# A gated long convolution and token MLP on one core: the k·v branch ahead of the filter, separate shuffle places, and a new fixed order

## The chip, the core and the metric

The kernel runs on one core of a Trainium2 chip. The core has a matrix engine (TensorE, PE), three engines for elementwise work (VectorE or DVE, ScalarE or ACT, GpSimd or POOL) and a sync engine (SP) that here only issues DMAs. The engines share an on-chip memory (SBUF, here one tensor named `arena`) and take matmul results from PSUM (`ps`, eight banks). Every engine runs its own list of instructions in a fixed order; semaphores hold an instruction until what it needs is done. The metric is device time in microseconds.

## The reference

The input x = A_q is 2048 tokens by 448 channels in bf16. Two blocks follow one another, each with a residual connection.

```python
# block A, on q = layernorm(x)
k_shift = sum over t in 0..3 of shift(k, t) * shift_k[:, t]     # causal, 4 taps, per channel
kv = k_shift * v
y  = irfft(rfft(kv, 4096) * rfft(ssm_k, 4096))[:2048]           # causal convolution of length 2048, per channel
h  = x + q * (y + kv * ssm_D)
# block B, over the tokens
u  = gelu(einsum("bsd,sf->bdf", layernorm(layernorm(h)), w1) + b1)   # f = 1792
out = h + transpose(einsum("bdf,fs->bds", u, w2) + b2)
```

## The kernel before

**The long convolution** is a Fourier transform of 4096 points (odd frequencies) written as matmuls. Tokens lie as 128 partitions by 16 rows. Both `kv` (the "u" branch) and the filter `ssm_k` (the "k" branch) go through the same steps:

1. *Stage 1* (`emit_stage1`, matmuls L1049): 16 steps per branch, each eight 32-row matmuls with a table `E` into two PSUM banks, then one eviction of 128 x 896 elements by ACT or DVE (L1059; L1057 for the first k group, which also adds `ssm_D`). The eviction writes a staging place (`GR_`). Four steps fill one place.
2. *Shuffle*: after every second step three DMAs (L1065; two issued by POOL, one by SP) carry the staged data to other partitions, into `TK` for k or `TU` for u.
3. *Stage 2* (`emit_stage2`, matmuls L1084) with the table `FW`; evictions L728, L729, L731, L732 write `TK` or `TU` in place.

Then `emit_products_i1` forms four products per frequency on DVE (L1150) and the first inverse stage on PE (L1167), evicted again by L728 and L731. DMAs L1190 shuffle the result into `TZ`. `emit_i2` (L1289, L1297) ends the inverse transform, gates with the normalised q, adds up statistics and writes the normalised rows `Q`. The MLP follows: L1422 is the first matmul for 7 of 14 column blocks, L1432 for the other 7 (ACT applies gelu, L1412), L1444 the second matmul, row by row, with L1447 on DVE and output DMAs L1452 to L1458.

**What feeds the two branches.** The k branch needs the filter's four channel chunks (load L877 into `KN`) transposed by PE (L1028) and evicted into `KT`. The u branch needs all of k (L888), transposed (L956) and evicted into `KX`; a short convolution on PE (L982) with a table `DG`, which DVE makes (L941) from the shift weights (loads L880 and L883, cast on POOL L934); and v (L891), which DVE multiplies in (L997). The table `E` is made on DVE (L827 product, L831 add, L834 mask) and ACT (sine, L837), in two halves of eight rows. The q path loads X (L905), takes statistics on DVE (L1226, L1228) and the reciprocal root on POOL (L1234, L1237).

**Places.** Four staging places form a ring, `gring`; the eight groups of the two branches take them as they come free. Two of them lie where X goes later and two where the product buffers (`MR`) go. X is loaded after all shuffles of u. The filter, `KN`, lies in the place of `TU`.

**What sets the order.** The program is planned when it is built. Every helper records its operations with a list of what they read and write. Each step, such as "stage 1 of u, step 5", takes a rank from the table `WHEN`. A list scheduler with an estimated duration for each operation then walks through time: whenever an engine is free it takes, among the operations that are ready, the one with the smallest rank. `WHERE` says for an eviction whether ACT (a), DVE (d) or either (f) may do it. The result is one fixed order per engine, and the waits are put in from the recorded reads and writes. A DMA is an operation of the queue that issues it, so an issue that waits holds what stands behind it.

Of the kernel before, what the change touches and what calls it, by code (L numbers as in the profile page):

```python
# [7 lines left out]
ALU = mybir.AluOpType  # L8
# [4 lines left out]
    "dummy": (54,),  # L13
    "tables": (137, 107, 179, 164, 70, 80, 73, 176,),
    "loads": (106, 111, 114, 115, 217, 195, 86, 237, 90, 235, 158, 197, 227, 143, 150,),
    "kv": (219, 110, 132, 216, 134, 214, 55, 208, 233, 84, 103, 104, 75, 127, 138, 154, 196,),
    "kT": (60, 57, 218, 64, 231, 198, 146, 78,),
    "k1": (109, 112, 145, 186, 105, 136, 139, 157, 61, 89, 100, 135, 92, 207, 161, 159,),
    "k2": (85, 88, 67, 87, 129, 141, 98, 155, 206, 203, 173, 175, 102, 113, 185, 247,),
    "u1": (68, 81, 99, 116, 131, 147, 144, 169, 172, 174, 210, 229, 65, 97, 140, 223,),  # L20
    "xload": (287, 46, 43, 49,),
    "bias": (193, 277,),
    "q": (213, 278, 298, 222, 309, 50, 94, 204, 279,),
    "u2": (72, 83, 209, 220, 156, 192, 82, 63, 96, 151, 149, 133, 53, 56, 291, 221,),
    "ew": (244,),
    "i1": (272, 29, 45, 194, 122, 263, 123, 91, 128, 273, 148, 265, 71, 74, 38, 189, 126,),
    "ct0": (188, 288,),
    "ct": (225, 3, 302,),
    "xn": (5, 17, 93, 39, 125, 261,),
    "w1a": (205, 303, 163, 286,),  # L30
    "warm": (41, 2,),
    "i2": (304, 9, 299, 58, 124, 22, 66, 234, 79, 305, 1, 160, 108, 23, 13, 310, 21, 42, 162, 6, 202, 10, 120, 18,
        69, 295, 19, 184, 27, 20, 142, 101, 306, 292, 34, 32, 255, 11, 165, 51, 289, 153, 224, 200, 301, 52, 187,
        177, 238, 199, 269, 280, 300, 226, 259, 118, 180, 31, 7, 170, 215, 117, 166, 167, 276, 181, 232, 307, 33,
        296, 4, 76, 77, 14, 182, 283, 168, 30, 293, 95, 47, 152, 12, 183, 270, 28, 37, 16, 40, 171, 36, 308, 44, 239,
        130, 15, 62, 119, 212, 228, 274, 24, 258, 25, 59, 35,),
    "w1b": (211,),
    "w2": (249,),
    "mlp": (190, 240, 8, 178, 297, 26, 48, 201, 290, 230, 121, 0, 241, 243, 275, 242, 260, 294, 418, 419, 420, 421,
        422, 423, 424, 425, 426, 427, 428, 429, 430, 431, 432, 433, 434, 435, 436, 437, 438, 439,),  # L40
}
WHERE = {
    "kv": "ddaadfdd",
    "kT": "ddfdfddd",
    "k1": "faffaffadfaa",
    "k2": "addfffdaffdafffd",
    "u1": "fafdffafafddfffa",
    "bias": "f",
    "u2": "aadafafafaaaffaf",
    "i1": "aaaaffafaaafaffa",  # L50
    "ct0": "d",
    "ct": "fda",
    "xn": "ffff",
    "i2": "afffaaffddfd",
# [89 lines left out]
class _Sched:  # L144
# [161 lines left out]
    def schedule(self):  # L306
# [70 lines left out]
        while done < n:  # L377
            progressed = False
            for e in ENGS:
                if free_at[e] <= t + 1e-9 and ready[e]:  # L380
# [34 lines left out]
                    if o.is_dma:  # L415
                        d0 = free_at[e] + (1200.0 if o.rate != 425.0 else 2000.0)
                        s = max(d0, fab)
                        fab = s + o.nbytes / o.rate
                        fin = max(fab, s + o.nbytes / (o.keng * 27.2))
                        fin += 600.0  # L420
                    else:
                        fin = free_at[e] + self.lat[e]
# [150 lines left out]
def _build(nc, A_q, A_k, A_v, A_shift_k, A_ssm_k, A_ssm_D, B_w1, B_b1, B_w2, B_b2, out):  # L573
# [36 lines left out]
    o_KN = o_TU  # L610
# [17 lines left out]
    with ctx:  # L628
# [53 lines left out]
        o_GR = (o_WR, o_WR + 8 * DB, o_X, o_X + 8 * DB)  # L682

        def GR_(s):
            return view(o_GR[s], [R // 4, 2, D])
# [13 lines left out]
        gring = _Pool(4)  # L699
# [9 lines left out]
        def Pbf(b, i, dt_=bf16):  # L709
            return PS[:, b.slots[i], :].bitcast(dt_)  # L710
# [26 lines left out]
        def emit_tables():  # L737
# [85 lines left out]
            for h in range(2):  # L823
                sch.t0 = T_TH if h else -40.0
                o_ph = (o_pi, o_TK)[h]
                ph = view(o_ph, [2, 8, 128], i32)
                op("dve", lambda e, W, h=h, ph=ph: e.tensor_tensor(  # L827
                    out=ph[:, 1], in0=frow.unsqueeze(1).broadcast_to([128, 8, 128]),
                    in1=srow[:, 8 * h:8 * h + 8].unsqueeze(2).broadcast_to([128, 8, 128]), op=ALU.mult),
                   r=[(o_fr, 512), (o_s, 64)], w=[(o_ph + 4096, 4096)], n=HALF, kind="1x")  # L830
                op("dve", lambda e, W, ph=ph: e.tensor_scalar(  # L831
                    out=ph[:, 0], in0=ph[:, 1], scalar1=2048, scalar2=None, op0=ALU.add),
                   r=[(o_ph + 4096, 4096)], w=[(o_ph, 4096)], n=HALF)
                op("dve", lambda e, W, ph=ph: e.tensor_scalar(  # L834
                    out=ph, in0=ph, scalar1=8191, scalar2=None, op0=ALU.bitwise_and),
                   r=[(o_ph, 8192)], w=[(o_ph, 8192)], n=2 * HALF)
                op("act", lambda e, W, h=h, ph=ph: e.activation(  # L837
                    out=E[:, 16 * h:16 * h + 16, :].rearrange("p a (b c f) -> p a b c f", b=4, c=2).rearrange("p a b c f -> p (a b) c f"),
                    in_=ph.rearrange("p c r (g f) -> p c (r g) f", f=16).rearrange("p c g f -> p g c f"),
                    func=ACT.Sin, bias=bias[:, 0:1], scale=-SC),  # L840
                   r=[(o_ph, 8192), (o_b, 4)], w=[(o_E + 4096 * h, 4096)], n=2 * HALF)
# [31 lines left out]
        def emit_loads():  # L873
            Dq = "sp"
            for i, c in enumerate((0, 1, 2, 3)):
                sch.t0 = -20.0 + i
                op(Dq, lambda e, W, c=c: e.dma_start(KN[0:CW[c], c, :], A_ssm_k[128 * c:128 * c + CW[c], :]),  # L877
                   w=[(o_KN + 4096 * c, 4096)], dmab=CW[c] * 4096, rate=217.0 if c == 3 else None)
            sch.t0 = -15.0
            op(Dq, lambda e, W: e.dma_start(wsn[:, 0:3], A_shift_k[0:384].rearrange("(c p) j -> p c j", p=128)),  # L880
               w=[(o_wsn, 24, "ws")], dmab=3072)
            for h in range(2):
                op(Dq, lambda e, W, h=h: e.dma_start(wsn[64 * h:64 * h + 64, 3], A_shift_k[384:448]),  # L883
                   w=[(o_wsn + 24, 8, "ws")], dmab=512)
            for i, (src, c) in enumerate((("k", 3), ("k", 0), ("v", 0), ("k", 1), ("v", 1), ("k", 2), ("v", 2), ("v", 3))):
# [13 lines left out]
               dmab=F * 2, keng=14)  # L899
            op(Dq, lambda e, W: e.dma_start(b2n, B_b2.rearrange("(q r) -> q r", r=R)), w=[(o_b2n, 32)], dmab=S * 2)  # L900

        def emit_xload():
            for c in range(4):
                sch.t0 = T_XL + c
                op("sp", lambda e, W, c=c: e.dma_start(X[:, 4 * c:4 * c + 4, :], x2d[:, 4 * c:4 * c + 4, :]),  # L905
                   w=[(o_X + 4 * c * DB, 4 * DB)], dmab=128 * 4 * DB,
                   after=shuf["u"])
# [24 lines left out]
        def emit_kv():  # L932
# [3 lines left out]
            for i in range(2):  # L936
# [7 lines left out]
               r=[(o_I2, 128), (o_wsc, 64)], w=[(o_DG, 2048)], n=1024, est=1700.0)  # L944
# [75 lines left out]
        def emit_kT():  # L1020
            k = None
            for i, c in enumerate((0, 1, 2, 3)):
                cw = CW[c]
                for g in range(2):
                    sch.t0 = T_KT + 1.0 * (2 * i + g)
                    b = _Buf(psum)
                    for rr in range(8):
                        k = op("pe", lambda e, W, b=b, rr=rr, r=8 * g + rr, c=c, cw=cw: e.transpose(  # L1028
                            out=Pbf(b, 0)[:, rr * cw:rr * cw + cw], in_=KN[0:cw, c, r:S:R], identity=ID[0:cw, 0:cw]),
                            r=[(o_KN + 4096 * c, 4096), (o_ID, 256)], bw=[b], kind="tr", mode=4 if c == 3 else 0,  # L1030
                            safter=(k,) if c == 3 and rr == 0 else ())
                    evac(lambda g=g, c=c, cw=cw: KT[:, 8 * g:8 * g + 8, 128 * c:128 * c + cw],
                         lambda b=b, cw=cw: Pbf(b, 0)[:, 0:8 * cw].rearrange("p (r d) -> p r d", r=8),
                         [(o_KT + r * DB + 256 * c, 2 * cw) for r in range(8 * g, 8 * g + 8)], b, 8 * cw,
                         est={"act": 60.0 + 0.824 * 8 * cw, "dve": 75.0 + 0.512 * 8 * cw})
# [3 lines left out]
        def emit_stage1(src, o_src, T, o_T, tag):  # L1039
            shuf[tag] = []  # L1040
            for i in range(R // 4):
                g = _Buf(gring)
                for jh in range(4):
# [10 lines left out]
                    def fn(e, W, b=b, g=g, jh=jh, i=i):  # L1054
                        dst = GR_(g.slots[0])[:, jh]
# [5 lines left out]
                    op("dve" if first else FX, fn, r=[(o_DR, DB)] if first else [], br=[b], bw=[g], n=2 * D, kind="psum")  # L1061
                    if jh % 2 == 0:
                        continue
                    for q_, a, nu in (("pool", 0, 8), ("pool", 96, 8), ("sp", 32, 16)):
                        shuf[tag].append(op(q_, lambda e, W, g=g, i=i, a=a, nu=nu, jh=jh: e.dma_start(  # L1065
                            T[a + i:a + i + 4 * nu - 3:4].rearrange("p (j k) c d -> p j k c d", k=4)[:, :, jh - 1:jh + 1]
                            .rearrange("p j k c d -> p j (k c d)"),
                            GR_(g.slots[0])[a:a + 4 * nu, jh - 1:jh + 1].rearrange("p k c d -> p (k c d)")),
                           br=[g], w=[(o_T + (4 * j + jh - 1) * 2 * DB, 4 * DB, tag) for j in range(4)],
                           dmab=4 * nu * 4 * DB, keng=nu, rate=350.0))  # L1070
                wbufs.append(g)

        wbufs = []
# [66 lines left out]
        def emit_products_i1():  # L1140
            for jj in range(R // 2):
                ms = []
                for h in range(2):
# [5 lines left out]
                    aft = [x for w in wbufs for x in w.readers] if i == 0 else [mfirst[0]]  # L1149
# [357 lines left out]
```

## Time and profile before

| | |
|---|---|
| runs, median (lowest to highest) | 177.0 us (176.32 to 177.84), 3 runs |
| span of the profiled execution | 173.7 us; its device time is not given apart, the median lies 3.3 us above |
| busy over the span | PE 161.4, DVE 103.1, ACT 89.7, POOL 58.8 us |
| granted TensorE clock | 1.000 |
| bytes moved by DMA | 35.15 MB, mean 202 GB/s |
| shuffle L1065: issue on POOL, median issue to landing | 0.553 us, 3.4 us |
| stage 1 eviction of 128 x 896: ACT, DVE | 0.913 us, 1.085 us (single records, which overlap by some 0.1 us) |
| product L1150 on DVE | 16 times, 1.08 us each |

A record of PE overlaps the next one, since matmuls are pipelined: 352 ns are shown for a 448-column matmul that follows another after 189 ns. So the distance between starts is what counts there. "Idle before, and releaser" in a line of the profile says how long an engine stood still before an instruction and what ended it.

### The profile page before, as it was taken

The page shows a single profiled execution, that of the slowest core. Times are in us where ns is not written, and L with a number is a line of the kernel's source. Part 1 is how long each engine was busy: PE and PEld are TensorE (multiplying, and loading weights), DVE is VectorE, ACT ScalarE, POOL GpSimd, SP SyncE. Part 2 cuts the span into 40 slices and gives each one's busy share as a digit, 9 for nine tenths or more (in the row PEclk, how much of TensorE's full clock was granted, in tenths as well). Part 3 has the DMA queues.
Part 4 walks back from the last instruction along what each step waited for, and adds up shares of the span by engine and source line. Part 5 has one row for each costly group of instructions (what it writes and reads, how often), then busy time and mean ns, then how long its engine had stood idle before and what let it go on. Part 6 is the DMA issues. An engine that isn't in the chain of part 4 may idle for free.

```text
span 173.7 us, 3570 instructions
## 1 busy us (share of the span) xinstructions
PE 161.4 (93%) x1419; PEld 92.1 (53%) x1419; DVE 103.1 (59%) x191; ACT 89.7 (52%) x129; POOL 58.8 (34%) x152
## 2 busy tenths in 40 slices
PE   6989999979989999838999999999999999999994
PEld 2766745442333332424345555555567777777783
DVE  7997899868979999979897751000002132231231
ACT  3796757798999999878883455421120000000000
POOL 8345717680912524564989640000000000000000
PEclk9999999999999999999999999999999999999999
DMA  5999865783859668755999999930000111101111
GB/s 163 408 299 380 284 177 213 301 330 117 244 113 389 198 193 258 246 168 166 392 396 402 416 423 421 417 150 0 0 0 4 53 53 53 44 9 57 53 53 53
DMA packets 15628, 35.15 MB, mean 202 GB/s; under 512 B 3740, under 2 KB 9740, under 8 KB 15612
## 3 DMA queue, kind: packets, MB, share of 16 engines
q1 hardware_dynamic: 12468, 28.25, 44.7%
q0 software_dynamic: 2880, 6.49, 11.4%
q8 instruction: 11, 0.18, 0.4%
q10 hardware_dynamic: 264, 0.18, 0.3%
q14 instruction: 5, 0.04, 0.1%
HBM read 22.05 MB, written 1.84 MB: 137 GB/s over the span
## 4 chain that ended last, share of the span: by engine, by line
PE 61%; DVE 11%; DMA 10%; ACT 8%; POOL 5%; issue 2%; SPq 1%; DVEq 0%; ACTq 0%; POOLq 0%
PE ps L1444 24%; PE ps L1432 12%; PE ps L1422 9%; DMA arena<-arena 6%; DVE arena L1150 5%; DMA arena<-in_A_ssm_k_dram 5%; ACT arena L1059 4%; PE ps L1084 3%; ACT arena L728 3%; PE ps L1049 3%; PE ps L982 2%; PE ps L1167 2%; PE ps L1028 2%; DVE arena L1226 2%; ACT arena L729 2%
## 5 line engine op out<-in xcount | busy, mean ns | idle before, releaser
L1447 DVE SCALAR_TENSOR_TENSOR arena<-ps,arena 128x448 bf16<-128x448 f32 (+2 forms) x17 | 11.1, 656 | 55.7 <-PE ps L1444 55.7
L1444 PE MATMUL ps<-arena 128*128 128x448 bf16 (+2 forms) x238 | 42.7, 342 | 0.0
L1444 PEld LDWEIGHTS ps<-arena 128*128 128x128 bf16 x238 | 33.3, 145 | 9.5
L728 ACT CAST arena<-ps 128x896 bf16<-128x896 f32 (+1 forms) x31 | 24.9, 943 | 1.1 <-PE ps L925 0.6
L1422 PE MATMUL ps<-arena 128*128 128x448 bf16 x112 | 23.1, 353 | 0.9 <-DVE arena L1364 0.6
L1059 ACT CAST arena<-ps 128x896 bf16<-128x896 f32 x23 | 19.5, 913 | 6.6 <-PE ps L1049 6.5
L1065 POOL DMA_DIRECT2D arena<-arena x32 | 17.5, 553 | 13.3 <-ACT arena L1059 12.6
L1432 PE MATMUL ps<-arena 128*128 128x448 bf16 x112 | 21.7, 352 | 0.0
L1084 PE MATMUL ps<-arena 128*64 128x448 bf16 x128 | 16.0, 361 | 1.8 <-ACT arena L1059 0.9
L1412 ACT ACTIVATE arena<-ps,arena 128x448 bf16<-128x448 f32 x14 | 8.2, 640 | 17.5 <-PE ps L1432 15.1
L1150 DVE TENSOR_TENSOR arena<-arena 128x1792 bf16<-128x1792 bf16 x16 | 16.6, 1081 | 0.9 <-DMA arena<-arena 0.9
L1422 PEld LDWEIGHTS ps<-arena 128*128 128x128 bf16 x112 | 10.5, 98 | 12.2 <-DVE arena L1375 3.0
L1432 PEld LDWEIGHTS ps<-arena 128*128 128x128 bf16 x112 | 11.0, 98 | 10.2
L1167 PE MATMUL ps<-arena 64*128 64x448 bf16 x128 | 14.3, 351 | 1.8 <-DVE arena L1150 0.8
L1049 PE MATMUL ps<-arena 128*32 128x448 bf16 x256 | 15.1, 355 | 0.6 <-DVE arena L997 0.3
L1190 POOL DMA_DIRECT2D arena<-arena x14 | 8.2, 589 | 16.4 <-ACT arena L728 16.4
L1344 ACT ACTIVATE arena<-arena 128x448 bf16<-128x448 f32 x14 | 8.1, 575 | 7.1 <-DVE arena L1316 6.9
L1084 PEld LDWEIGHTS ps<-arena 128*64 128x64 f16 x128 | 5.4, 108 | 11.4 <-ACT arena L728 3.8
L1167 PEld LDWEIGHTS ps<-arena 64*128 64x128 f16 x128 | 5.0, 94 | 10.9 <-ACT arena L728 5.3
L1289 PE MATMUL ps<-arena 128*128 128x448 bf16 x32 | 7.7, 353 | 2.6 <-DMA arena<-arena 2.6
L731 DVE COPY arena<-ps 128x1024 bf16<-128x1024 bf16 (+2 forms) x15 | 9.2, 648 | 0.6 <-PE ps L1028 0.6
L1049 PEld LDWEIGHTS ps<-arena 128*32 128x32 f16 x256 | 5.0, 95 | 8.4 <-DVE arena L997 2.6
(96 smaller groups left out, 190.3 us busy)
## 6 DMA issues: line engine op xcount, KB each, us to landing
arena<-in_B_w_dram SPq DMA_DIRECT2D x8, 896.0 KB, 10.3
arena<-in_B_w_dram SPq DMA_DIRECT2D x2, 2048.0 KB, 17.5
arena<-arena SPq DMA_DIRECT2D x16, 224.0 KB, 3.4
arena<-arena POOLq DMA_DIRECT2D x32, 112.0 KB, 3.4
arena<-in_B_w_dram SPq DMA_DIRECT2D x2, 1536.0 KB, 18.9
arena<-arena POOLq DMA_DIRECT2D x14, 196.0 KB, 4.2
arena<-in_A_k_dram SPq DMA_DIRECT2D x4, 448.0 KB, 6.0
arena<-in_A_v_dram SPq DMA_DIRECT2D x4, 448.0 KB, 9.2
```

What stands on the lines that cost most here:

```text
L728: return e.copy(out=dst(), in_=src())
L731: return e.tensor_copy(out=dst(), in_=src())
L1049: op("pe", lambda e, W, b=b, r=r, q=q, x=x, c0=c0: e.matmul(PS[32 * q:32 * q + 32, b.slots[x], 0:D], E[:, 2 * r + x, c0:c0 + 32], src[:, r ...
L1059: return e.copy(out=dst, in_=Ppair(b)) if W == "act" else e.tensor_copy(out=dst, in_=Ppair(b))
L1065: shuf[tag].append(op(q_, lambda e, W, g=g, i=i, a=a, nu=nu, jh=jh: e.dma_start(T[a + i:a + i + 4 * nu - 3:4].rearrange("p (j k) c d -> p ...
L1084: op("pe", lambda e, W, b=bs[h], h=h, j=j, c=c, par=par: e.matmul(PS[64 * par:64 * par + 64, b.slots[c], 0:D], FW[:, 64 * c:64 * c + 64], ...
L1150: op("dve", lambda e, W, m=m, i=i: e.tensor_tensor(out=MR(m.slots[0]).rearrange("p (x y) d -> p x y d", x=2), in0=TU[:, i].unsqueeze(2).br ...
L1167: k = op("pe", lambda e, W, b=bs[h], m=ms[h], par=par, t=t, tab=tab, xy=xy, P=P: e.matmul(Pb(b, par), tab[P, :], MR(m.slots[0])[P, xy, :], ...
L1422: op("pe", lambda e, W, r=r, fc=fc, b=bs[fc]: e.matmul(Pb(b), W1A[:, r, 128 * fc:128 * fc + 128], Q[:, r, :], start=(r == 0), stop=(r == R ...
L1432: op("pe", lambda e, W, r=r, fc=fc, b=b: e.matmul(Pb(b), W1B[:, r, 128 * (fc - n0):128 * (fc - n0) + 128], Q[:, r, :], start=(r == 0), sto ...
L1444: op("pe", lambda e, W, r=r, fc=fc, b=b, d0=d0, d1=d1: e.matmul(Pb(b)[:, d0:d1], W2[fc // 7][:, fc % 7, r:S:R], G[:, fc, d0:d1], start=(fc ...
L1447: op("dve", lambda e, W, r=r, b=b, A=A, d0=d0, d1=d1: e.scalar_tensor_tensor(out=X[:, r, d0:d1], in0=Pb(b)[:, d0:d1], scalar=bm[:, r:r + 1 ...
```

## The change

- **Loads.** Filter chunk 3 (64 channels) is loaded as two halves of 1024 tokens each, one on partitions 0 to 63 issued by SP, one on partitions 64 to 127 issued by ACT; the transposes of that chunk are done for each half apart. The shift weights are loaded by ACT's queue instead of SP's. `KN` moves from the place of `TU` into the back of the place of `TK`.
- **Staging.** The ring of four is replaced by eight fixed places, four for u and four for k. u's are the old four. k's lie in `TZ` and in the place of raw k. X no longer waits for all of u's shuffles, but for those that read its own part.
- **Tables.** The add of 2048 goes from DVE to POOL, the mask and the sine are cut into two halves each.
- **Planner.** The estimate for making `DG` goes from 1700 to 1150 ns, and a transfer takes at least 190 ns in the plan.
- **Order.** All ranks and engine choices are new. By the new ranks, SP's first loads come in this order: filter chunk 0, k pieces 2, 1, 3, 0, filter chunk 2, v 2, v 3, v 1, `b1`, `ssm_D`, filter chunk 1, filter chunk 3 (first half), `b2`, v 0; before: k 0, k 1, filter 0 to 3, `ssm_D`, biases, k 2, k 3, v 2, weights, v 3, v 1, v 0. In the second matmul of the MLP the rows were done in order, 0 to 15; now in the order 9, 10, 14, 3, 11, 5, 13, 6, 8, 0, 1, 4, 12, 2, 7, 15.

```diff
 WHEN = {
...
-    "loads": (106, 111, 114, 115, 217, 195, 86, 237, 90, 235, 158, 197, 227, 143, 150,),
-    "kv": (219, 110, 132, 216, 134, 214, 55, 208, 233, 84, 103, 104, 75, 127, 138, 154, 196,),
-    "kT": (60, 57, 218, 64, 231, 198, 146, 78,),
-    "k1": (109, 112, 145, 186, 105, 136, 139, 157, 61, 89, 100, 135, 92, 207, 161, 159,),
+    "loads": (36, 286, 173, 305, 138, 113, 97, 157, 312, 49, 199, 42, 183, 187, 277, 266, 311,),
+    "kv": (70, 93, 35, 165, 290, 99, 261, 275, 214, 126, 96, 14, 72, 13, 61, 73, 150,),
+    "kT": (310, 169, 21, 140, 189, 7, 248, 17,),
+    "k1": (60, 103, 37, 197, 237, 131, 293, 19, 137, 159, 271, 268, 54, 28, 134, 251,),
...
-    "u1": (68, 81, 99, 116, 131, 147, 144, 169, 172, 174, 210, 229, 65, 97, 140, 223,),
-    "xload": (287, 46, 43, 49,),
+    "u1": (203, 132, 98, 79, 233, 291, 95, 89, 8, 81, 200, 142, 270, 82, 74, 76,),
+    "xload": (239, 108, 111, 83,),
...
-    o_KN = o_TU
+    o_KN = o_TK + 12288
...
-        o_GR = (o_WR, o_WR + 8 * DB, o_X, o_X + 8 * DB)
+        o_GR = {"u": (o_WR, o_WR + 8 * DB, o_X, o_X + 8 * DB), "k": (o_TZ, o_TZ + 8 * DB, o_KH, o_KH + 8 * DB)}
...
-        gring = _Pool(4)
...
-                op("dve", lambda e, W, ph=ph: e.tensor_scalar(
-                    out=ph[:, 0], in0=ph[:, 1], scalar1=2048, scalar2=None, op0=ALU.add),
...
+                op("pool", lambda e, W, ph=ph, raw=raw: e.tensor_scalar(
+                    out=ph[:, 0], in0=raw, scalar1=2048, scalar2=None, op0=ALU.add),
...
+                for x in (1, 0):
+                    op("dve", lambda e, W, ph=ph, raw=raw, x=x: e.tensor_scalar(
+                        out=ph[:, x], in0=raw if x else ph[:, 0], scalar1=8191, scalar2=None, op0=ALU.bitwise_and),
...
-            for i, c in enumerate((0, 1, 2, 3)):
-                sch.t0 = -20.0 + i
-                op(Dq, lambda e, W, c=c: e.dma_start(KN[0:CW[c], c, :], A_ssm_k[128 * c:128 * c + CW[c], :]),
...
+            for h in range(2):
+                sch.t0 = -17.0 + 0.1 * h
+                op("act" if h else Dq, lambda e, W, h=h: e.dma_start(
+                    KN[64 * h:64 * h + 64, 3, 0:S // 2], A_ssm_k[384:448, S // 2 * h:S // 2 * h + S // 2]),
...
-            op(Dq, lambda e, W: e.dma_start(wsn[:, 0:3], A_shift_k[0:384].rearrange("(c p) j -> p c j", p=128)),
+            op("act", lambda e, W: e.dma_start(wsn[:, 0:3], A_shift_k[0:384].rearrange("(c p) j -> p c j", p=128)),
...
-                   w=[(o_X + 4 * c * DB, 4 * DB)], dmab=128 * 4 * DB,
-                   after=shuf["u"])
+                   w=[(o_X + 4 * c * DB, 4 * DB)], dmab=128 * 4 * DB)
...
-                    aft = [x for w in wbufs for x in w.readers] if i == 0 else [mfirst[0]]
+                    aft = wr_out if i == 0 else [mfirst[0]]
```

## The prediction

> **What bounds the kernel now.** I read the span by stages first (the table of stretches: length, then busy time and instruction count of PE, PE's weight loads, DVE, ACT and POOL, granted clock, DMA share, GB/s).
>
> ```profile
> 0.00:20.00 20.00, 18.00 (x237) 11.81 (x239) 17.39 (x34) 13.64 (x15) 11.87 (x57) 1.00 0.91 308
> 20.00:48.40 28.40, 26.50 (x470) 12.69 (x466) 24.91 (x33) 22.57 (x28) 16.51 (x32) 1.00 0.68 233
> 48.40:73.50 25.10, 22.64 (x206) 8.48 (x205) 24.18 (x38) 24.71 (x30) 8.61 (x18) 1.00 0.72 234
> 73.50:77.00 3.50, 0.87 (x17) 0.70 (x14) 3.50 (x11) 2.16 (x3) 2.97 (x7) 1.00 0.58 187
> 77.00:90.70 13.70, 12.84 (x64) 5.74 (x64) 11.70 (x38) 12.38 (x28) 9.32 (x20) 1.00 0.84 299
> ```
>
> Up to 73.5 us the scarce thing is the pair DVE and ACT, which empty PSUM: from 48.4 to 73.5 they work 24.2 and 24.7 of 25.1 us. Before that they leave 2.6 + 6.4 us (to 20) and 3.5 + 5.8 us (20 to 48.4) unused. PE's "busy" says little here: the records overlap. The clock is 1.00 throughout. Second view, the chain that ended last (start, length, what):
>
> ```profile
> 71.84 0.58 POOL arena L1190
> 72.42 4.51 DMA arena<-arena
> 76.98 0.55 PE ps L1289 x2
> ...
> 108.28 20.43 PE ps L1432 x108
> 128.71 42.08 PE ps L1444 x231
> 170.82 0.55 DVE arena L1447
> ```
>
> The last inverse shuffle is issued at 71.8, lands at 76.9, and PE starts i2. In the unbroken stretch a 448-column matmul costs 20.43 / 108 = 0.189 us. The 64 matmuls of 77.0 to 90.7 need 12.1 us of these 13.7, so PE loses only 1.6 us there, and nothing after 90.7. So the end is: end of the front + 4.5 (shuffle) + 92 us of matmul + 1.6 + tail. The change touches no matmul of that tail, so **nearly all it can win or lose lies ahead of 73.5**. Third view, who waited for whom (total us, times, longest):
>
> ```profile
> ACT arena L1059 <- PE ps L1049: 6.5, 7, 2.6
> ACT arena L728 <- PE ps L956: 3.1, 1, 3.1
> POOL arena L934 <- DMA arena<-in_A_shift_k_dram: 1.2, 1, 1.2
> DVE arena L1059 <- PE ps L1049: 1.4, 2, 0.8
> ```
>
> The evictions of stage 1 (L1059) wait for its matmuls (L1049). Those of the u branch need conv(k)·v, whose products (L997) start at 20.7 and end at 40.4, because the shift weights land only at 15.8 (L934) and DVE has the filter's evictions to do meanwhile. So the second branch trickles; its last eviction ends at 44.5 and its last shuffle lands at 50.2, where SP is released to load X.
>
> **The change, part by part.**
>
> *Loads and new order.* By the new ranks SP issues filter chunk 0, k (four pieces), filter chunk 2, v2, v3, v1, then filter chunk 1, half of chunk 3, and v0. The first load landed 4.0 us after its issue at 0.73, the next two 448-512 KB pieces 1.1 and 1.2 us later each. So k is complete near 9.3 (now 13.8: issue 5.8 + 8.0), v2 near 11.8 (now 18.6), filter chunk 1 near 15.5, v0 near 17. The weights go to ACT's queue near 1 to 2 us: with 4.0 to 8.5 us to landing (the fastest first load, the slowest weights) they land at 5 to 10.5; I take 8. The convolution (now from 19.6) can start near 11, the u branch's first eviction falls near 14, where the k branch's first one is now (14.7). The filter is transposed by 17.5 to 18; from there all 16 evictions of the k branch are ready at once. That is the point: the branch with two steps ahead of it goes first, and the second no longer trickles. ACT's four issues at about 0.5 us end near 2.7; with the table load (1.28) ACT is free at 4.2, and it waits for transposes until 5.6 now: cost nothing. Without that cover: 2 us on ACT, 1 us on the pair.
>
> *Eight staging places, k's and u's own.* The view of waits has no row of an eviction waiting for a staging place, so what goes is 0 to 0.6 us (the idle before the eviction at 34.50, where the chain has a shuffle of 5.07 us ahead). I take 0. What it moves is the load of X: it waited for all u shuffles and was issued at 50.28. Now each piece waits for its own half of u's staging, perhaps near 25 to 35, and L1226 can fill gaps:
>
> ```profile
> L1226 DVE BATCH_NORM_STATS2 arena<-arena 128x6 f32<-128x448 bf16 x9 | 5.2, 608 | 0.0
> L831 DVE TENSOR_SCALAR arena<-arena 128x1024 int32<-128x1024 int32 x2 | 1.4, 685 | 0.0
> L844 POOL TENSOR_SCALAR arena<-arena 128x128 int32<-128x128 int32 x3 | 2.0, 689 | 2.7 <-DVE arena L821 2.7
> L848 POOL TENSOR_TENSOR arena<-arena 128x384 int32<-128x384 int32 x1 | 1.0, 994 | 0.1
> ```
>
> 5.2 us of it now stand inside the saturated stage. Each X transfer is also queued on SP ahead of shuffles (below).
>
> *Tables.* DVE loses two L831 (1.4 us). ACT's two sines of 2048 become four of 1024: the rows 384 in 0.62 and 2048 in 2.02 give 0.33 us fixed, so + 0.7. Net 0.7 less on the pair, 0.35 us of time. POOL gets two adds of 1024: copies of 48 and 288 elements take 0.23 and 0.44, which gives 1.0 to 1.1 each; memset of 1024 takes 0.95; L844 scaled by length would be 5.5. I take 1.1, nearest in kind per element; at 5.5 the sines end near 17 instead of 12, where stage 1 wants them at 14: + 3 us.
> The Trainium skill (SBUF — State Buffer, "Who interferes with whom") says that a DVE instruction in a two-port mode and a GpSimd instruction block each other for a whole instruction; by it these adds could hold back a mask on DVE by an add each, an estimate of 1 to 2 us of DVE, and the table move would bring nothing. No row here isolates it.
>
> *Filter's last chunk on both halves.* 16 more transposes; the present sixteen ran in 1.18 us, so 0 to 1.2 us of PE, which has gaps there (0.62 at 10.7). I take 0. The present 64-partition load landed 1.0 us after the 512 KB before it for half the bytes; from 9 to 11 us only about 195 GB/s flow against 415 just before, 0.4 MB lost, so 0 to 1 us of transfer may be won. It is among the last loads: 0 taken, since the engines then have u work.
> On this the Trainium skill (DMA: Bandwidth & Descriptors, "Rules for kernel authors") says that splitting into partition halves is not worth it, since both halves share the same engines and serialise: by it 0, by the row up to 1 us.
>
> *Sum.* Of the 18.3 us that DVE and ACT leave unused before 48.4, about 5 belong to the start (nothing has landed), so 13 can be filled. Work that fills them is there from 14 us on. I take half, as each engine's order is still fixed beforehand: 6.5 / 2 = 3.2, plus 0.35: **3.6 us** earlier at 73.5. DMA allows it: loads 5.5, shuffles 7.3, X 1.8 MB at 400 GB/s are 36.5 us from 3, so 39.5, against 50.2. POOL allows it: 32 issues at 0.553 are 17.7 us from 15. Span 173.7 - 3.6 = 170.1; the median of the runs is 3.3 above the profiled span (its own device time is not given), so **173.4**.
>
> **Tail.** The new ranks put the rows 9, 10 and 14 of the last matmul ahead of most W1 columns. Now W2 is first used at 128.5 and its pieces land at 103.4 to 116.0; then row 9 starts right after the W1A part ends (108.3 now). First two pieces: 103.4 and 107.2. The cover shrinks from over 20 us to about 1 to 5, still not negative: 0. At 2 us later loads: up to 1 us.
>
> **Rivals.** *The front is filled completely:* 6.5 + 0.4 and the 1.6 after 77 us, since the statistics are done early: 177.0 - 8.5 = 168.5. Against: no stage before 48.4 came near.
> *The order moves, the end does not:* filter chunk 0 is still first, k's evictions are simply last instead of u's, and they end near 44 as now. Gain only from L831 and moved statistics, against 1 us of holds: 175.3 to 178.7, middle 177. For it: the amount of work is the same.
> *X ahead of the filter's shuffles (slower):* an X issue waits on SP for u's shuffles to land (2.2 to 5.1 us) and holds k's shuffles queued behind it; then its 1.8 MB take 4.6 us of the DMA engines, which were at 0.9 or more from 29 to 32 and 37 to 40. If nothing else is won, the last shuffle lands at 54.8 instead of 50.2; the stage after it is 5.2 / 2 = 2.6 shorter: + 2.0, **179.0**; with a longer hold 180. It decides once k's last shuffle lands after 52.8. Against: DMA stood idle from 24.4 to 27.4 and 40.4 to 44.
>
> **Numbers.** Forecast (171.5 to 175.2) 0.45; full 0.13; no move 0.20; X in the way, or late tables, 0.22. A measurement of this kernel tells about 1%, 1.8 us, from no change. Faster 0.58, same 0.20, slower 0.22. Range 168.5 to 179.8: full filling to the held X; about 0.15 outside, most above. The forecast's own range is 171.5 to 175.2.
>
> **What would show it.** Right: products (L997 now) done by about 20 instead of 40.4; k's last shuffle lands near 46.6; X issued before 40; the last inverse shuffle issued near 68, i2 near 73.4; no PE gap before the last matmuls. Wrong: gaps of DVE plus ACT between 20 and 48 still near 9 us, k's stage 1 waiting for filter chunk 1 after 18, SP waiting ahead of X, or PE idle for W2.

## The result, and the profile after

| | before | changed |
|---|---|---|
| median (lowest to highest), 4 runs each on one chip | 177.42 us (176.32 to 177.88) | 183.86 us (182.50 to 186.93) |
| ratio, 95% interval | | 1.0376 [1.0282, 1.0469] |
| profiled execution: its time, span | span 173.7 us | 184.08 us, span 182.3 us |
| first i2 matmul (end of the front) | 76.98 us | 84.76 us |
| end of PE | 170.82 us | 179.40 us |

The change makes the kernel **3.8% slower**; 173.4 us had been forecast and 179.8 was the upper end of the range. On another chip, beside other runs of before, the changed kernel gave 1.0382 [1.0274, 1.0489] (run e0, below). A median here is over all runs; a ratio leaves out runs that lie more than 1.5% above the fastest of the same kernel. Of the 8.6 us by which PE ends later, 7.8 stand ahead of i2 and 0.8 behind it.

First the table of stretches of the changed kernel, in the columns of the one shown of before. The stage of the products stood at 48.4 to 73.5 there and stands at 59.0 to 81.9 here.

```profile
0.00:20.00 20.00, 13.98 (x178) 10.28 (x180) 13.94 (x27) 11.39 (x13) 16.30 (x54) 0.91 0.77 277
20.00:40.00 20.00, 19.41 (x383) 11.64 (x377) 17.00 (x28) 13.69 (x17) 8.20 (x16) 1.00 0.51 168
40.00:59.00 19.00, 15.56 (x184) 5.38 (x176) 16.62 (x23) 16.12 (x21) 12.26 (x24) 1.00 1.02 300
59.00:81.90 22.90, 20.13 (x197) 8.31 (x194) 22.75 (x32) 22.65 (x30) 9.23 (x17) 1.00 0.49 143
```

Three things are to be seen. In the first 20 us DVE and ACT leave 6.1 + 8.6 us unused, against 2.6 + 6.4 before, while POOL's busy time rises from 11.9 to 16.3. From 40 to 59 us the DMA engines are full (1.02) and DVE and ACT leave 2.4 + 2.9 us. And the last stage of the front is 22.9 us long, hardly shorter than before (50.3 to 73.5, measured likewise from the first product to the last eviction, is 23.2), though eight of X's sixteen statistics were done ahead of it, none before.

Then the chain that ended last (start, length in us, what; some pieces left out at each "..."):

```profile
4.40 2.43 POOL arena L832
7.71 3.29 POOL arena L832
...
12.23 1.23 DVE arena L948
13.45 1.21 DVE arena L730 x2
14.71 1.25 PE ps L989 x20
...
49.28 6.99 DMA arena<-arena
...
81.96 5.34 DMA arena<-arena
```

Before, this chain began with the filter's load (2.58 to 10.71) and held a shuffle of 5.07 us. Now its first long pieces are the two adds on POOL (L832); it goes on with `DG` (L948) and the convolution (L989), and holds a shuffle of k that takes 6.99 us.

The adds by themselves (the view of one line: duration in ns min/median/max, first and last start), and what DVE and PE do around them (timelines):

```profile
L832 POOL TENSOR_SCALAR arena<-arena x2: 3232/3258/3285, 4.4 to 7.7; 128x1024 int32<-128x1024 int32 x2
```
```profile
4.87 1.00 DVE L817 TENSOR_TENSOR arena<-arena 128x1 int32<-128x1 int32 x1
...
7.67 0.69 DVE L836 TENSOR_SCALAR arena<-arena 128x1024 int32<-128x1024 int32 x1 [0.92 <-POOL arena L832]
...
11.03 0.69 DVE L836 TENSOR_SCALAR arena<-arena 128x1024 int32<-128x1024 int32 x1 [1.50 <-POOL arena L832]
12.23 1.23 DVE L948 TENSOR_TENSOR arena<-arena 128x1024 bf16<-128x1024 bf16 x1 [0.50 <-POOL arena L941]
```
```profile
9.02 0.62 PE L963 MATMUL ps<-arena 128*128 128x128 bf16 x8 [2.29 <-DVE arena L730]
13.51 0.28 PE L989 MATMUL ps<-arena 64*128 64x256 bf16 x2 [1.95 <-DVE arena L948]
```

An add takes 3.26 us on POOL; before, DVE did the same work in 0.685 us (L831). Behind the adds stand on POOL the cast of the shift weights (L941), which had landed at 7.4 and were cast at 12.0; on DVE the masks, with the evictions of the transposes queued behind them; and behind those PE, which stands still twice. After these gaps the records show the clock at 0.5 for 3.4 us (14.5 to 17.9):

```profile
PEclk9996999999999999999999999999999999999999
```

That is so in this execution, and not in each one. The profiled execution of e2 (below) has the same order and starts the convolution at the same 13.51 us, but its clock stays at 1.00. From 14.71 us on its PE is ahead, and stage 1 of u (L1060) starts 1.4 us earlier. First the changed kernel, then e2:

```profile
14.71 1.25 PE L989 MATMUL ps<-arena 64*128 64x64 bf16 x22
21.59 0.56 PE L1060 MATMUL ps<-arena 128*32 128x448 bf16 x8
```
```profile
14.71 0.73 PE L989 MATMUL ps<-arena 64*128 64x64 bf16 x22
20.19 0.56 PE L1060 MATMUL ps<-arena 128*32 128x448 bf16 x8
```

So whoever takes this trace as the measure finds 1.4 us of half clock in the 7.8. That matters below, as the profiled runs of e1, e2, e3 and e7 all have the full clock there.

At the other end of the front, the shuffles (the view of line L1077, as the two lines of its answer; before, the median to landing was 3.4 us and the last issue 46.2):

```profile
L1077 POOL DMA_DIRECT2D arena<-arena x32: 544/544/808, 25.9 to 56.5; - x32
...
DMA to landing us min/median/max: 2.5/5.3/8.6
```

### The profile page after: what moved, and what is told of

Same layout as the page of the kernel before. It is cut to its first block, busy times and chain, and to the rows that moved or that the text cites. A ratio compares the mean times of both kernels' runs of the same rounds, so it can differ in the third digit from the quotient of the medians.

```text
span 182.3 us, 3598 instructions
## 1 busy us (share of the span) xinstructions
PE 163.4 (90%) x1435; PEld 93.5 (51%) x1435; DVE 104.8 (58%) x190; ACT 92.4 (51%) x132; POOL 65.7 (36%) x154
## 4 chain that ended last, share of the span: by engine, by line
PE 56%; DMA 14%; DVE 12%; ACT 9%; POOL 4%; issue 3%; DVEq 0%
PE ps L1457 23%; PE ps L1445 11%; DMA arena<-in_B_w_dram 7%; DMA arena<-arena 7%; PE ps L1435 7%; PE ps L1060 4%; ACT arena L727 3%; DVE arena L1163 3%; POOL arena L832 3%; ACT arena L728 3%; PE ps L989 3%; PE ps L1037 3%; PE ps L1180 2%; ACT arena L1070 2%; DVE arena L1004 2%
## 5 line engine op out<-in xcount | busy, mean ns | idle before, releaser
L1457 PE MATMUL ps<-arena 128*128 128x448 bf16 (+2 forms) x238 | 44.2, 342 | 0.0
L1457 PEld LDWEIGHTS ps<-arena 128*128 128x128 bf16 x238 | 32.6, 145 | 10.9 <-ACT arena L1425 2.0
L1425 ACT ACTIVATE arena<-ps,arena 128x448 bf16<-128x448 f32 x14 | 8.9, 634 | 31.2 <-PE ps L1445 24.9
L1435 PE MATMUL ps<-arena 128*128 128x448 bf16 x112 | 24.6, 353 | 0.0
L1077 POOL DMA_DIRECT2D arena<-arena x32 | 17.7, 557 | 18.2 <-ACT arena L1070 13.9
L1445 PE MATMUL ps<-arena 128*128 128x448 bf16 x112 | 23.3, 352 | 0.7 <-DMA arena<-in_B_w_dram 0.7
L727 ACT CAST arena<-ps 128x896 bf16<-128x896 f32 (+1 forms) x25 | 21.4, 925 | 2.7 <-PE ps L1097 1.8
L1070 ACT CAST arena<-ps 128x896 bf16<-128x896 f32 x20 | 17.3, 911 | 6.1 <-PE ps L1060 6.0
L1097 PE MATMUL ps<-arena 128*64 128x448 bf16 x128 | 15.4, 359 | 3.9 <-DMA arena<-arena 1.7
L1445 PEld LDWEIGHTS ps<-arena 128*128 128x128 bf16 x112 | 10.9, 98 | 11.0 <-DVE arena L1388 1.1
L1060 PE MATMUL ps<-arena 128*32 128x448 bf16 x256 | 15.3, 356 | 1.0 <-ACT arena L727 0.4
L1435 PEld LDWEIGHTS ps<-arena 128*128 128x128 bf16 x112 | 10.6, 98 | 10.5 <-DVE arena L1388 1.6
L727 ACT COPY arena<-ps 128x1024 bf16<-128x1024 bf16 (+2 forms) x13 | 12.4, 981 | 2.2 <-PE ps L963 1.6
L728 ACT ACTIVATE arena<-ps 128x896 bf16<-128x896 f32 x12 | 10.8, 965 | 0.6 <-PE ps L1097 0.6
L1239 DVE BATCH_NORM_STATS2 arena<-arena 128x6 f32<-128x448 bf16 x16 | 9.5, 613 | 2.0 <-DMA arena<-in_A_q_dram 1.9
L1302 PE MATMUL ps<-arena 128*128 128x448 bf16 x32 | 7.7, 353 | 2.8 <-DMA arena<-arena 2.5
```

Source lines behind the costliest of these rows:

```text
L727: return e.copy(out=dst(), in_=src())
L728: return e.activation(out=dst(), in_=src(), func=ACT.Copy, scale=scale)
L1060: op("pe", lambda e, W, b=b, r=r, q=q, x=x, c0=c0: e.matmul(PS[32 * q:32 * q + 32, b.slots[x], 0:D], E[:, 2 * r + x, c0:c0 + 32], src[:, r ...
L1070: return e.copy(out=dst, in_=Ppair(b)) if W == "act" else e.tensor_copy(out=dst, in_=Ppair(b))
L1077: shuf[tag].append(op(q_, lambda e, W, i=i, a=a, nu=nu, jh=jh: e.dma_start(T[a + i:a + i + 4 * nu - 3:4].rearrange("p (j k) c d -> p j k c ...
L1097: op("pe", lambda e, W, b=bs[h], h=h, j=j, c=c, par=par: e.matmul(PS[64 * par:64 * par + 64, b.slots[c], 0:D], FW[:, 64 * c:64 * c + 64], ...
```

## The experiments

Each run's time is a median, given with that of before on the same chip. "Frozen" means that the planner's list of operations is kept, and only the engine of the operation named is exchanged when the program is written; a new plan would move everything at once.

**e0: the changed kernel once more.** No edit.

> The changed kernel itself, unchanged, on the chip of these runs, so that the others can be set against it. All theories: 1.03 to 1.045 of the kernel before.

184.48 us, ratio 1.0382 [1.0274, 1.0489] to 175.83.

**e1: the two adds back on DVE, order frozen.**

```diff
                 op("pool", lambda e, W, ph=ph, raw=raw: e.tensor_scalar(
...
-                   r=[(o_rw, 4096)], w=[(o_ph, 4096)], n=HALF, est=1050.0)
+                   r=[(o_rw, 4096)], w=[(o_ph, 4096)], n=HALF, est=1050.0, force="dve")
```

> The changed kernel with its planned order frozen; only the two adds of 2048 are issued by DVE instead of POOL, at the same place of the order. Theory A (the two adds of 3.26 us hold POOL, behind them the cast of the shift weights, and DVE's masks with the evictions queued behind them): the table DG is ready near 8.5 instead of 13.45, the first u eviction starts near 16 instead of 22.3, k's last shuffle lands near 51 instead of 56.3, time near 178.5 (5 us less than 183.9). Theory B (X's transfers ahead of the k shuffles are the loss): the head may move, but k's last shuffle still lands after 54, time 182 or more. Theory C (the new order alone is the loss, whatever the adds cost): first u eviction earlier, time still 182 or more.

181.39 us, ratio 1.0238 [1.0132, 1.0344] to 176.42. The clock is at 1.00, the first shuffle is issued at 22.9 instead of 25.9, and i2 starts at 81.94 instead of 84.76: **2.8 us**. As 1.4 of these are the half clock of the other trace, an estimated 1.4 are left for the adds themselves. The 5 us that had been expected did not come; what is left of the loss stands around X. Its chain (lines of e1 are two higher than those of the changed kernel):

```profile
31.59 5.11 DMA arena<-arena
...
36.71 5.22 DMA arena<-in_A_q_dram
...
46.96 7.13 DMA arena<-arena
```

A shuffle of u is waited for, then a piece of X, and then a shuffle of k takes 7.13 us.

**e2: a quarter of X's bytes.** The adds stay on POOL, and so do the four issues of X with their waits; each loads one row of four.

```diff
-  op("sp", ... e.dma_start(X[:, 4 * c:4 * c + 4, :], x2d[:, 4 * c:4 * c + 4, :]),
+  op("sp", ... e.dma_start(X[:, 4 * c:4 * c + 1, :], x2d[:, 4 * c:4 * c + 1, :]),
```

> The changed kernel in its order, but each load of X brings one row of four, 0.46 MB instead of 1.84 MB; three quarters of X are left out and the statistics read what lay there. Theory B (X ahead of k's shuffles): the median landing of the shuffles falls from 5.3 to about 3.4 us, k's last shuffle lands near 53, time near 181. Theory A (adds on POOL): nothing before 30 us changes, k's last landing stays within 1 us of 56.3, time 183 or more.

181.52 us, ratio 1.0291 [1.0231, 1.0351] to 176.42. i2 starts at 80.61, 4.2 us earlier. But stage 1 of u is already 1.4 us ahead, before the first load of X is issued (29.8): that is the clock again. An estimated **2.8 us** are left for X. PE ends 2.4 us earlier (176.96 instead of 179.40): of the rest, 1.1 go to the wait for the MLP's weights, which is 1.8 us here and 0.7 in the changed kernel. The shuffles now land after 4.0 us (median):

```profile
L1077 POOL DMA_DIRECT2D arena<-arena x32: 544/544/808, 24.5 to 52.4; - x32
...
DMA to landing us min/median/max: 2.2/4.0/7.1
```

The waits of the X issues on SP are still there. So what goes is the share of X's bytes in the DMA engines, and the waits of those who need X.

**e10: the same quarter in before** (control).

> The kernel before with X's loads cut to one row of four (three quarters of X left out), as a control for what fewer bytes of X bring by themselves. There X is loaded after all shuffles, so all theories expect 0.995 to 1.003 of the kernel before. A larger gain would mean that the gain of the changed kernel with a quarter of X is not due to the place of its load.

176.27 us, ratio 1.001 [0.9968, 1.0052] to 175.83. Where X comes behind all shuffles, as before, its bytes cost nothing that can be measured.

**e3: e1 and e2 together.**

> The changed kernel in its frozen order with both edits: the adds of 2048 on DVE, and X's loads cut to one row of four (three quarters of X left out). If the two causes are separate, the gains add: about 1.4% and 0.9% off 1.038, so 1.013 to 1.018 of the kernel before (178.7 to 179.6 against 176.4), i2 starts near 78 instead of 84.8. If they are two faces of one wait, the time is that of the better of the two alone, 1.024. If nothing but these two was lost, as my forecast implies, it would be at 0.98.

179.30 us, ratio 1.0191 [1.0133, 1.0249] to 175.83; i2 at 79.69. Ahead of i2 the traces gain 2.8 and 4.2 us apart and 5.1 together; at the end of PE 2.8 and 2.4 apart and 4.9 together (174.48). The 1.4 us of the half clock are in each of these figures. Counted once, the rest adds up: ahead of i2 1.4 + 1.4 + 2.8 = 5.6 (in e3 a matmul of stage 1 comes 0.8 late, for no reason that the trace shows), and at the end, with the 1.1 us of e2's wait for weights put back, 1.4 + 1.4 + 2.1 = 4.9. The interval of e3's ratio lies clear below that of the changed kernel; those of e1 and e2 overlap with it, so apart each gain rests on one pair of traces. 2.7 us ahead of i2 and 3.7 at the end of PE remain. The stretches of e3:

```profile
0.00:20.00 20.00, 15.69 (x225) 11.08 (x226) 17.64 (x34) 12.33 (x14) 9.60 (x52) 1.00 0.80 277
20.00:40.00 20.00, 19.39 (x362) 10.88 (x363) 16.58 (x25) 14.71 (x19) 9.89 (x18) 1.00 0.57 184
40.00:54.50 14.50, 13.24 (x148) 4.57 (x148) 14.40 (x21) 14.06 (x18) 10.59 (x22) 1.00 0.90 270
54.50:77.60 23.10, 20.19 (x196) 8.31 (x195) 22.84 (x33) 22.75 (x29) 9.33 (x17) 1.00 0.50 146
```

Up to the end of i1 (73.5 before, 77.6 here) DVE and ACT leave 19.6 us unused before and 19.9 here. So the waiting is back at its old sum; the **busy time** has grown, from 66.5 + 60.9 to 71.5 + 63.9 us, by 7.9 engine-us, which is 3.9 us of time (from there to i2 it is 2.1 us here and 3.5 before, which leaves the 2.7). This is an accounting; what makes it up follows in the section on why.

**e7: the plan told the truth.** The adds stay on POOL, but the planner reckons 3260 ns for one and plans anew.

```diff
-                   r=[(o_rw, 4096)], w=[(o_ph, 4096)], n=HALF, est=1050.0)
+                   r=[(o_rw, 4096)], w=[(o_ph, 4096)], n=HALF, est=3260.0)
```

> The changed kernel with one number changed: the planner is told that an add on POOL takes 3260 ns instead of 1050, and plans anew with the same ranks; the adds stay on POOL. Theory A1 (the loss comes from the wrong estimate, work was put behind the adds that need not wait): 1.020 to 1.028 of the kernel before. Theory A2 (it is the place: the masks, sines and the cast need the adds, whatever the plan knows): 1.034 or more.

180.71 us, ratio 1.0284 [1.021, 1.0359] to 175.83; i2 at 80.11. POOL's timeline shows what the new plan did:

```profile
4.40 3.24 POOL L832 TENSOR_SCALAR arena<-arena 128x1024 int32<-128x1024 int32 x1
7.71 0.20 POOL L941 CAST arena<-arena 128x16 f32<-128x16 bf16 x1
...
10.59 2.79 POOL L832 TENSOR_SCALAR arena<-arena 128x1024 int32<-128x1024 int32 x1
```

The cast of the weights slips in between the adds, and `DG` is made at 8.96 instead of 12.23. The adds are as slow as ever. This points to what the plan had put behind the adds, on the strength of 1.05 us, as most of their cost. It does not show it: the plan is another one in other places too, 1.4 of the 4.7 us by which i2 comes earlier are the clock's, and the interval of the ratio holds what either theory expected.

**e4: only the adds of before on POOL, order frozen.**

```diff
                 op("dve", lambda e, W, ph=ph: e.tensor_scalar(
...
-                   r=[(o_ph + 4096, 4096)], w=[(o_ph, 4096)], n=HALF)
+                   r=[(o_ph + 4096, 4096)], w=[(o_ph, 4096)], n=HALF, force="pool")
```

> The kernel before in its planned order, frozen; only its two adds of 2048 go from DVE to POOL, as in the changed kernel. Theory A: each add takes about 3.3 us, the masks behind them on DVE and the evictions behind these wait some 3 us, the last sine ends near 15 instead of 12.1, time 179.5 to 181 against 177.4. Theories B and C: within 1 us of 177.4, since order and loads are as before.

183.13 us (179.55 to 184.04) against 176.42. The runs differ by their clock, so no ratio is given: the one at a mean clock of 0.99 took 179.55 us (+3.1), the three at 0.962 to 0.972 took 183.0 to 184.0 (+6.6 to 7.6). In the profiled one (mean clock 0.962), DVE's masks wait for the adds and PE for DVE; half the clock is then granted for 10.2 us:

```profile
4.52 2.80 POOL L833 TENSOR_SCALAR arena<-arena 128x1024 int32<-128x1024 int32 x1
```
```profile
7.36 1.29 DVE L836 TENSOR_SCALAR arena<-arena 128x2048 int32<-128x2048 int32 x1 [1.39 <-POOL arena L833]
11.66 1.23 DVE L836 TENSOR_SCALAR arena<-arena 128x2048 int32<-128x2048 int32 x1 [2.87 <-POOL arena L833]
```

All four runs lie above every run of before beside them (174.59 to 176.77), the one at 0.99 by some 3 us over the median of before, whose runs stood at 0.99 to 1.00. So the adds alone make the old kernel slower as well. How much of that is the adds and how much the clock stays open.

**e9: PE kept busy across its gap.** Ten matmuls on a dummy tile stand ahead of the first of the convolution.

```diff
+            if self.fill and oid in self.fill[2]:
+                for _ in range(self.fill[0]):
+                    self.issue("pe", self.fill[1](self.eng["pe"]))
+                self.fill = None
...
+        sch.fill = (10, lambda e: e.matmul(Pb(dumb), DUM[:, 0:128], DUM, start=True, stop=True), conv)
```

> The changed kernel in its order with ten more 448-column matmuls on idle data, put on PE just ahead of the first convolution matmul, where PE stood idle from 11.6 to 13.5 us. Theory D (the idle PE brings the granted clock to half from 14.8 to 18.2 us, and this costs 1.7 us of PE in the chain): the clock stays at 1.00, the first u eviction starts near 20.5 instead of 22.3, time near 182.4. Otherwise: clock or time unchanged, 183.9 within 1 us.

183.06 us, ratio 1.0385 [1.0324, 1.0446] to 176.42. In three of the four runs the mean clock was back at 0.999 or 1.0, and the time stayed (182.6 to 183.2). By these runs the half clock costs nothing. But that is not settled. The profiled run is the fourth (186.45, mean clock 0.982): there half the clock is granted from 9.1 to 12.5 us, the ten matmuls end late, and the convolution starts at 14.97 instead of 13.51. And other figures speak against e9: the 1.4 us between the traces of the changed kernel and of e2, and two single runs at a mean clock of 1.000, one of e0 (181.63) and one of e12 (180.90), each 2 us or more below the runs of the same kernel at 0.991. What the half clock costs in time stays open, between nothing and some 2 us.

It is not the main part of the loss. Before, too, ran at 0.99 in 8 of the 13 runs beside e0; in the other five, at 0.999 or more, it took 174.6 to 175.7 us, and the one run of the changed kernel at 1.000 took 181.63.

**s1 and s2: ranks and engine choices searched anew** by the same random search with the program's own planner, for the new structure (s1: adds on DVE and reckoned there) and for the old one (s2), both with shuffles reckoned to land 0.8 us later. The edit of s1, of all new ranks and engine choices only the first:

```diff
 WHEN = {
-    "dummy": (252,),
+    "dummy": (170.84,),
...
-                        fin += 600.0
+                        fin += 1400.0 if o.rate == 350.0 else 600.0
...
-                op("pool", lambda e, W, ph=ph, raw=raw: e.tensor_scalar(
+                op("dve", lambda e, W, ph=ph, raw=raw: e.tensor_scalar(
```

> The changed kernel's loads, eight staging places and split last chunk, with the adds of 2048 on DVE and told to the planner as such, a shuffle's planned landing 0.8 us later, and ranks and engine choices searched anew (55 minutes of random exchanges against the planned end). Theory F (my forecast: the new structure frees 3.6 us, the loss is the adds and the order): 0.975 to 0.99 of the kernel before, i2 starts near 73.5. Theory E (the structure frees nothing, ranks decide): 0.995 to 1.015, the same as the next kernel within 1%.

> The kernel before, with the same 0.8 us for a shuffle's landing in the plan and ranks and engine choices searched for the same time in the same way. It shows what such a search gives without the new structure. Theory F: 0.995 to 1.015 of the kernel before, behind the other by 1.5% or more. Theory E: as the other, within 1%.

s1 took 180.88 us, 1.0252 [1.0168, 1.0336] to 176.06; s2 179.44 us, 1.0172 [1.0083, 1.026]. Both are slower than before, and their medians above what either theory had. What the pair tells: with equal effort on the order, the structure with eight places, early X and split chunk does not come out ahead; and a fresh order for the *old* structure loses 1.7%, about as much as what remained in e3 (1.9%). The order of before is hard to equal.

**e12: the rows of the second matmul in order again**, all ahead of them as in the changed kernel.

```diff
-    "mlp": (229, 158, ... 59, 84, 175, 225, 23, 112, 193,
-        161, 223, 247, 258, 292, 174, 274, 185, 240, 298, 241, 41, 45, 180, 278, 226, 75, 299,),
+    "mlp": (229, 158, ... 59, 84, 418, 419, 420, ... 438, 439, 440,),
```

> The changed kernel with the ranks of the last two parts of the MLP as in the kernel before (W1's second half, then the rows of the last matmul 0 to 15); all that is planned ahead of them stays the same, instruction by instruction. If the new row order costs something (PE waiting for weights, 0.7 us in the changed kernel's waits; the tail is 0.8 us longer than before): 1.030 to 1.035 of the kernel before. If it is free, as my prediction put it: 1.038 within 0.003.

183.21 us, ratio 1.0374 [1.0286, 1.0463] to 176.06: the row order can't be told from nothing in the time. In the trace it is 0.8 us. From the first i2 matmul to the end of PE it is 93.84 us in before, 93.84 in e12 (84.57 to 178.41) and 94.64 in the changed kernel, where one wait stands that e12 does not have (waits of PE from 88 us on):

```profile
PE ps L1445 <- DMA arena<-in_B_w_dram: 0.7, 1, 0.7
```

## Why the prediction was wrong

Of the 7.8 us that i2 comes later in the traces, 1.4 are the half clock, an estimated 1.4 the adds on POOL, 2.3 to 2.8 the place of X, and 2.7 what remains in e3. The 3.6 us that had been forecast as a gain are not found anywhere.

**What bounds the kernel: right.** The product stage is saturated after as before (22.75 and 22.65 of 22.9 us), and from the first i2 matmul to the end of PE it is 93.8 us before and 94.6, 94.7 and 94.8 us in the changed kernel, e1 and e3. Only e2 has 96.4, with its longer wait for weights.

**Step "tables": mis-sized, and the first cause.** The adds were taken at 1.1 us, between bounds of 0.95 and 5.5; they take 3.26. The row that decided was "nearest in kind per element", copies and a memset. The better row was in the same fence: L844, the one int32 operation with a scalar that POOL did, 689 ns for 128 elements. The 5.5 scaled from it was too much, but on the right side. At 5.5 a loss of 3 us was worked out, from the sines. The loss that came (2.8 us in the trace of e1, half of it the clock) went another way: through POOL's own queue. Step by step: the weights landed at 7.4, as foreseen (5 to 10.5, 8 taken). They were then cast at 12.0, because the cast stood behind both adds. The convolution started at 13.5 instead of 11, and the first eviction of u's stage 1 on ACT at 22.3 instead of 14. The prediction named DVE and ACT as the pair that counts and gave POOL's issues a line, but never asked what is queued behind the adds.

On the block of DVE by POOL, the Trainium skill (SBUF — State Buffer, "Who interferes with whom") says that whichever of the two issues first holds the shared ports for its whole instruction, and the other blocks fully. The trace agrees in part. The two-input L817 at 4.87, one element per partition, took 1.00 us while the first add ran, and 0.15 at the same place in e1, where POOL had no add. But a mask at 5.79 (0.68 us) and the next L817 at 6.39 (0.15 us) ran inside the same add, which lasted to 7.63, and were not held. So the hold cost DVE 0.85 us, less than the estimate of 1 to 2 us, while the masks waited 2.4 us for the adds' data.

**Step "X moves": priced at nothing, and the second cause.** X was issued at 30.7 to 44.7, where 25 to 35 had been guessed. The sum had it fit, since bytes over bandwidth left 10 us free over the whole front. But bytes over the whole front say nothing of 40 to 56 us, where the DMA share is 1.01 to 1.03 and the shuffles, which the engines wait for, land after 5.3 us instead of 3.4. e2 gives an estimated 2.8 us for it at i2, the clock's share taken off; with the adds out of the way and the full clock in both traces, e1 and e3 differ by 2.25 at i2 and 2.1 at the end of PE. The rival "X ahead of the filter's shuffles" was the right one in sign and place: its test was k's last shuffle after 52.8, and it landed at 56.3. It was given 179.0 where 183.9 came, since it had a held queue and 4.6 us of transfer alone, and since it took 2.6 us off the next stage for the statistics. That stage became 0.3 us shorter.

**Step "sum": half of the 13 unused us filled. This step failed.** In e3, with both causes out, the unused time up to the end of i1 is 19.9 us against 19.6: nothing was filled. The branch "with two steps ahead of it" became the serial one: the v products ended at 33.2 (20 foreseen, 40.4 before). In e3 ACT is busy for 5.9 of the 10 us from 20 to 30 and waits for stage 1's matmuls, since the filter's transposes stand late in PE's order (their last block of 32 runs at 32.5). What the prediction did not look at is the other side, the busy sum. It took the work of the pair as fixed but for the table; it grew, since the new choices give work to the engine that takes longer for it. The groups of before, then those of e3 (busy us, mean ns):

```profile
L731 DVE COPY arena<-ps 128x1024 bf16<-128x1024 bf16 x11 | 7.1, 684 | 0.3 <-PE ps L1028 0.3
...
L728 ACT COPY arena<-ps 128x1024 bf16<-128x1024 bf16 x3 | 2.8, 1020 | 3.1 <-PE ps L956 3.1
```
```profile
L732 DVE COPY arena<-ps 128x1024 bf16<-128x1024 bf16 x6 | 3.8, 680 | 0.6 <-PE ps L1039 0.6
...
L729 ACT COPY arena<-ps 128x1024 bf16<-128x1024 bf16 x8 | 7.8, 1012 | 0.6 <-PE ps L965 0.5
...
L1072 ACT CAST arena<-ps 128x896 bf16<-128x896 f32 x20 | 17.3, 911 | 6.9 <-PE ps L1062 6.8
```

Copies of 1024 bf16 cost 0.68 us on DVE and 1.01 on ACT; before, DVE did 11 of 14, now 6. Evictions of 896 f32 cost 1.08 on DVE and 0.91 to 0.97 on ACT, by line; DVE did 18 of 80, now 24. Five copies and six evictions changed for the dearer engine make about 1.7 and 0.7 to 1.0 of the 7.9 engine-us. Four sines in the place of two cost 0.6 to 0.7, about as predicted (the two rows it used give 0.29 us fixed, not 0.33). The rest is more statistics and normalised rows done before this end, and `DG` at 2.01 instead of 1.22 us beside POOL's table work. That this busy time is what remains of the loss was **not tried by an edit**: it is read from the trace, and how much of e3's 1.9% it is stays open. s2 says only that another order of the old structure can lose as much.

**The smaller steps.** Staging: no row of after has an eviction waiting for a place; 0 as predicted for it alone, but the freedom of X that comes with it is the second cause. The filter's last chunk on both halves: not tried apart; no row shows a gain or a loss. Tail: 0 to 1 us was given for later weights; 0.7 us of wait came, 0.8 with e12. Clock: not foreseen; half of it for 3.4 us puts the changed kernel's trace back by 1.4 us, and what that is in the run times stays open.

**The rival "the order moves, the end does not"** had the part that was right about the sum: the same gaps as before. The chances for slower were 0.22, all of it for X or late tables. Both came, and nothing was priced for their coming together.

## What to carry over

Before a piece of work goes to an engine "with time to spare", find the row of the same operation and type on that engine, however short, and list what is queued behind it there; an estimate in a planner is a claim to be read like any other. A load that is set free early is priced in the stretch where it will run, by the DMA share there and by the small transfers beside it that engines wait for, not by bytes over the whole stage. And when an order is made anew, compare the busy sums by engine and shape too: filling gaps can win nothing if the work has gone to the engine that is slower at it. And before two traces are subtracted, their granted clocks are compared ahead of the place where the edit can act: a trace is one execution.

## What the runs showed of the hardware

- An int32 add of a constant on 128x1024 took 2.8 to 3.3 us on POOL and 0.685 us on DVE.
- DVE's two-input, one-element L817 took 1.00 us just behind the start of such an add, and 0.15 us later in the same add; `DG`, 1.23 us in the changed kernel, took 2.01 us in e1 and e3, where POOL did its table work beside it.
- After PE gaps of 2.29 and 1.95 us early in the run the clock was granted at 0.5 for 3.4 us, in e0 after 1.03 and 1.95 us as well; in e2, after 1.59 and 1.95 us, it stayed at 1.00. So these gaps alone do not tell whether it comes. In e4, behind a gap of 3.35 us, it was 0.5 for 10.2 us. In three of four runs with matmuls in the second gap (e9) the mean was 0.999 or more.
- 1.8 MB of X among the shuffles took their median landing from 4.0 us (e2, a quarter of the bytes) to 5.3 us.
